# A fused convolution and MLP kernel: the third group's second matmul in seven half products, and the fourth group's second tap made before its first

## The chip, the cores and the metric

The kernel runs on one core of a Trainium2 chip. The metric is the device time in microseconds (us) of one execution. Times of the kernel before are the median of three runs; beside them stands one execution taken by the hardware profiler, and its trace.

A core has engines that run side by side, each with its own instruction queue: TensorE (PE; matmuls into PSUM, eight banks of accumulators), VectorE (DVE), ScalarE (ACT), GpSimd (POOL) and SyncE (SP). SP and POOL also issue DMA transfers here[...]. An engine takes its instructions in order: one that waits holds up all behind it.

## The reference

The input x has 8 sequences of 4224 rows of 192 values. A causal convolution with 7 taps runs along each sequence; the 192 channels form 8 heads of 24, and each head has its own 7 tap weights (a softmax). Then comes a layer normalization over the 192 channels, a matmul to 768 channels, a ReLU, a matmul back to 192, and a residual sum:

```python
w = softmax(weight)                                   # 8 heads x 7 taps
y = einsum('hk,bskhg->bshg', w, windows(x))           # causal, 7 taps
mu, var = mean(y), mean((y - mu) ** 2)                # over the 192 channels
xn = (y - mu) / sqrt(var + 1e-6) * g_ln
out = y + maximum(xn @ w_ch1, 0.0) @ w_ch2            # 192 -> 768 -> 192
```

All is float32.

## The kernel before

**Groups.** The 33792 rows are taken in 18 groups (`groups`, L70). A group is `n` rows on each of 128 partitions: group 0 has 6, group 1 has 8, group 2 has 10, groups 3 to 17 have 16. In the text "the third group" is group 2 and "the fourth" group 3. The buffers are reused: two for loaded rows (`xg`), two for convolved rows (`y`), one each for the transposed rows (`yt`), the hidden layer (`room`), and the results of the second matmul (`cs`).

**What happens to a group.** `load_x` brings its rows in. `first_tap` makes y = tap 0 times x on ScalarE, one instruction for each head (L378). The other taps are one VectorE instruction for each tap and head (`conv`, L403), adding into y. For groups from 4 on, `second_tap` makes tap 1's product on ScalarE into a buffer `tb` (L389), and two accumulating DMAs from POOL add it to y (L392), so that `conv` starts with tap 2. VectorE transposes y in 32x32 blocks (`transpose`, L414) and takes its moments (`moments`, L434); POOL computes the reciprocal root (`root`). `store_y` writes y to the output, and the result of the second matmul is added to the output in memory by an accumulating DMA (`add_to_out`, L891), after ScalarE has scaled it row by row (`scale`, L884).

**Two forms of the matmuls.** In the plain form the first matmul is `up` (six hidden blocks; each is evicted from PSUM by a ScalarE instruction with the ReLU, L509) and the second is `down` (L753), whose results `park` copies to SBUF (L870). In the other form, a matrix product of 2x2 blocks is made of seven half-size products in place of eight, with sums of blocks before and after. `up_mixed` does so for the first matmul from group 3 on: it needs sums of quarters of w1 (`w1sums`, and w12 replaced by w12 - w11) and of the transposed rows (`sums_of_y`; its last two on POOL), and it closes some blocks by copying a partial product to SBUF and adding it there with an accumulating DMA from POOL (`close`, L585). `down_fast` does so for the second matmul: it needs sums of quarters of w2 (`w2sums`), sums of quarters of the hidden layer made by VectorE while the products run (`lower_sum`, `half_sum`, L773), and it copies blocks out on ScalarE (L812). Between the copies ScalarE does other work for later groups, so many pieces behind each copy (`behind`).

**Order.** It is written out by hand; each engine runs its instructions in the order in which the loop from L973 makes them. For groups 0 to 2 that order was: issue the load of group g + 2, `up(g)`, then convolution, transpose, moments and first taps of the groups ahead, then `down(g)`. The sums of w2's quarters stood on VectorE behind group 1's second matmul (L1006), and those of w1's behind group 2's (L1012). Group 2 used `down`; group 3 is the first in the other form for both matmuls. `fast` (L76) says how many rows of a group the second matmul takes in the seven-product form.

**The steps on which the order rests.** An eviction must end before TensorE refills its banks. In `up_mixed` a partial product lies in a part of `room` that a later copy overwrites, so that copy waits for the DMA that adds it. In `down_fast` the second half of the products reads the half sums.

## Time and profile before

| | |
|---|---|
| median of three runs | 962.16 us (959.97 to 962.44) |
| the profiled execution | 960.25 us |
| its span, first to last instruction | 958.5 us |
| granted TensorE clock in it | 0.999 |
| third group's first matmul (L519, 288 instructions of 320 columns) | 80.5 to 100.1 us |
| third group's second matmul (L753, 288 of 320) | 100.1 to 119.6 us |
| fourth group's first matmul (L519, 504 of 256) | 119.6 to 147.4 us |
| fourth group's second matmul (L806, 504 of 256) | 147.4 to 174.9 us |
| DMA: POOL's queue | 100.94 MB, 55.0% of 16 engines' span |
| DMA: SP's queue | 63.31 MB, 17.9% |

How to read it: a row of a timeline gives the start, the length, the engine, the line of the kernel, the operation, output and inputs with their shapes, how many instructions are merged, and in brackets how long the engine had idled and what ended that. Lengths of neighbours overlap a little; the time from one start to the next is what an instruction takes of its engine. A matmul here shows as two instructions. L numbers are lines of the kernel before.

### The profile page before, as it was taken

To read this page: it belongs to the slowest core of one execution; us is meant where nothing else is said; L and a number is where in the kernel's file an instruction comes from. 1 tells how busy PE (TensorE), PEld (TensorE's weight loads), DVE (VectorE), ACT (ScalarE), POOL (GpSimd) and SP (SyncE) were. 2 spreads that over 40 slices of the span, in tenths; PEclk is the share of its full clock that TensorE was granted. 3 is DMA by queue.
4 is the path that set the end of the run, shared out by engine and by line. 5 is a ranking of instruction groups with operands and counts; after the bars stand their busy time and mean duration, and the time that the engine had idled before them with its cause. 6 is when DMAs were issued, how large, how long until landed. Compare 5 with 4: busy or idle time off the path is not lost.

```text
span 958.5 us, 38499 instructions
## 1 busy us (share of the span) xinstructions
PE 948.6 (99%) x17274; PEld 719.5 (75%) x17274; DVE 895.8 (93%) x1510; ACT 686.6 (72%) x1139; POOL 260.9 (27%) x399
## 2 busy tenths in 40 slices
PE   8999999999999999999999999999999999999997
PEld 7886596776869687786958678686867768586787
DVE  8999998999999999999999999999989999999667
ACT  6625578596877959687796958778695877866461
POOL 1005311612135131422216131341315221161400
PEclk9999999999999999999999999999999999999999
DMA  8243887679697887969788796978879697767241
GB/s 221 79 155 112 180 207 216 146 151 265 134 260 142 235 173 158 249 123 276 136 240 163 178 234 118 281 136 243 158 186 216 120 280 141 179 132 129 53 83 68
DMA packets 28394, 166.69 MB, mean 174 GB/s; under 512 B 3397, under 2 KB 4294, under 8 KB 22215
## 3 DMA queue, kind: packets, MB, share of 16 engines
q0 software_dynamic: 21568, 100.94, 55.0%
q1 hardware_dynamic: 6656, 63.31, 17.9%
q8 instruction: 135, 2.21, 0.9%
q14 instruction: 29, 0.24, 0.1%
q10 hardware_dynamic: 6, 0.00, 0.0%
HBM read 38.93 MB, written 50.33 MB: 93 GB/s over the span
## 4 chain that ended last, share of the span: by engine, by line
PE 97%; ACT 1%; DMA 1%; DVE 0%; SPq 0%; issue 0%; ACTq 0%
PE ps L519 48%; PE ps L806 42%; PE ps L753 6%; DMA xg<-in_x_dram 1%; PE ps L322 1%; ACT w L360 0%; ACT room L618 0%; DVE y L898 0%; ACT spare L241 0%; ACT y L378 0%; PE ps L335 0%; SPq L215 0%; ACT room L509 0%; PE ps L350 0%; SPq L210 0%
## 5 line engine op out<-in xcount | busy, mean ns | idle before, releaser
L403 DVE SCALAR_TENSOR_TENSOR y<-xg,taps,y 128x384 f32<-128x384 f32 (+3 forms) x734 | 367.9, 577 | 1.8 <-issue 1.6
L519 PE MATMUL ps<-yt,w 32*128 32x256 f32 (+2 forms) x4104 | 235.7, 379 | 0.4 <-ACT room L509 0.4
L806 PE MATMUL ps<-room,w2sums 128*32 128x256 f32 (+1 forms) x4320 | 235.9, 375 | 0.0
L618 ACT COPY room<-ps 128x1024 f32<-128x1024 f32 (+1 forms) x135 | 175.0, 1296 | 77.2 <-PE ps L519 76.0
L519 PEld LDWEIGHTS ps<-yt,w 32*128 32x128 f32 x4104 | 204.2, 185 | 26.5 <-issue 9.0
L806 PEld LDWEIGHTS ps<-room,w2sums 128*32 128x32 f32 x4320 | 140.5, 110 | 89.7 <-ACT room L631 4.9
L806 PE MATMUL ps<-room,w 128*32 128x256 f32 (+1 forms) x3240 | 181.0, 375 | 0.4 <-issue 0.4
L773 DVE TENSOR_TENSOR room<-room 128x1024 f32<-128x1024 f32 (+1 forms) x135 | 151.6, 1196 | 21.2 <-PE ps L806 20.0
L806 PEld LDWEIGHTS ps<-room,w 128*32 128x32 f32 x3240 | 104.8, 110 | 68.7 <-DVE room L624 5.0
L519 PE MATMUL ps<-ysums,w1sums 32*128 32x256 f32 x2160 | 124.9, 379 | 0.0
L519 PEld LDWEIGHTS ps<-ysums,w1sums 32*128 32x128 f32 x2160 | 108.7, 185 | 11.2 <-ACT room L618 3.6
L812 ACT COPY cs<-ps 128x256 f32<-128x256 f32 (+1 forms) x180 | 66.0, 369 | 42.6 <-PE ps L806 42.6
L884 ACT ACTIVATE ot<-ot,r 128x192 f32<-128x192 f32 x232 | 93.8, 462 | 0.0
L631 ACT ACTIVATE room<-room 128x1024 f32<-128x1024 f32 (+1 forms) x89 | 92.1, 1071 | 0.0
L891 POOL DMA_DIRECT2D out_dram<-ot x40 | 34.2, 1086 | 194.6 <-ACT ot L884 115.7
L378 ACT ACTIVATE y<-xg,taps 128x384 f32<-128x384 f32 (+3 forms) x141 | 72.8, 611 | 9.0 <-DVE st L434 7.6
L434 DVE BATCH_NORM_STATS2 st<-y 128x6 f32<-128x192 f32 x264 | 70.2, 344 | 0.0
L519 PE MATMUL ps<-yt,w1sums 32*128 32x256 f32 x1080 | 65.1, 379 | 0.0
L812 ACT COPY room<-ps 128x256 f32<-128x256 f32 (+1 forms) x90 | 33.6, 373 | 43.9 <-PE ps L806 42.4
L519 PE MATMUL ps<-ysums,w 32*128 32x256 f32 x1080 | 64.5, 376 | 0.0
L618 ACT ACTIVATE room<-ps 128x1024 f32<-128x1024 f32 (+1 forms) x30 | 43.6, 1454 | 27.6 <-PE ps L519 27.6
L389 ACT ACTIVATE tb<-xg,taps 128x384 f32<-128x384 f32 x112 | 61.9, 635 | 0.0
(109 smaller groups left out, 895.3 us busy)
## 6 DMA issues: line engine op xcount, KB each, us to landing
xg<-in_x_dram SPq DMA_DIRECT2D x15, 2112.0 KB, 19.2
room<-room POOLq DMA_DIRECT2D x45, 512.0 KB, 5.3
out_dram<-ot POOLq DMA_DIRECT2D x29, 768.0 KB, 9.5
y<-tb POOLq DMA_DIRECT2D x28, 768.0 KB, 11.4
out_dram<-y SPq DMA_DIRECT2D x13, 1536.0 KB, 10.8
room<-parts_cs POOLq DMA_DIRECT2D x28, 512.0 KB, 6.6
room<-parts_tb POOLq DMA_DIRECT2D x14, 1024.0 KB, 7.6
xg<-in_x_dram SPq DMA_DIRECT2D x1, 1536.0 KB, 8.0
```

Source lines behind the costliest of these rows:

```text
L378: nc.scalar.mul(y[g][:, 0:n, cs], xg[g][:, 0:n, cs], taps[:, h, 0:1])
L389: nc.scalar.mul(tb[g][:, 0:n, cs], xg[g][:, 1 : 1 + n, cs], taps[:, h, 1:2])
L403: nc.vector.scalar_tensor_tensor(out=y[g][:, 0:n, cs], in0=t[:, k : k + n, cs], scalar=taps[:, h, k : k + 1], in1=y[g][:, 0:n, cs], op0=AL ...
L434: nc.vector.bn_stats(out=sums[g][:, j, :], in_=y[g][:, j, :])
L519: nc.tensor.matmul(banks[:, q, i * w : i * w + w], right[rows, c, P * i : P * i + P], left[rows, :, c, :], start=(first and c == 0 and i = ...
L618: nc.scalar.activation(dst, src, AF.Relu) if relu else nc.scalar.copy(dst, src)
L631: nc.scalar.activation(c, c, AF.Relu)
L753: nc.tensor.matmul(bank[C * q : C * q + C, 0:w], w2[:, f, C * c : C * c + C], left, start=(f == 0), stop=(f == NF - 1),)
L773: nc.vector.tensor_tensor(a[:, *dst, f], a[:, *left, f], a[:, *right, f], op=op)
L806: nc.tensor.matmul(dst[C * q : C * q + C, 0:w], right[:, f, C * c : C * c + C], left[:, f, q], start=(first and f == PAIR), stop=(f == PAI ...
L812: nc.scalar.copy(to[:, c], dst[:, 0:w].rearrange("p (j t) -> p j t", t=t))
L884: nc.scalar.mul(ots[g][:, j, :], ots[g][:, j, :], rstd[g][:, j : j + 1])
```

## The change

The third group's second matmul goes over to the seven-product form (`fast[2]`), with one ScalarE piece behind each copy of its first four products. Its first matmul keeps the plain form; only the layout in which its result is written differs.

- The sums of w2's quarters and most of w1's leave VectorE: ScalarE writes a negated quarter and accumulating DMAs from POOL add the others (`between`, between the hidden blocks of groups 1 and 2). Only w12 - w11 stays on VectorE.
- The second tap of group 2 and that of heads 0 to 5 of group 3 are made on ScalarE and added by DMA (`add_second_tap`). For group 3 it is made before the first tap, into a free end of `room`, while group 1's hidden blocks are evicted; the DMA moves 144 of each row's 192 channels.
- The loads of groups 3, 4 and 5 move: group 3's ahead of the stores of group 1 on SP, group 4's and 5's to POOL's queue. The load of group 5 and the store of group 3's y come behind the third group's second matmul.
- First taps of group 4 are made between hidden blocks of group 2; its second tap is made during the second matmul of group 2.
- The scaling of groups 0 and 1 and their additions to the output are regrouped. Group 2's result is finished as the later groups' are, inside the next group's first matmul.

```diff
@@ -75,6 +75,7 @@
 
     fast = {g: groups[g][2] if g >= 3 else 0 for g in range(NG)}
     fast[NG - 1] = J - 5
+    fast[2] = groups[2][2]
     NFAST = max(fast.values())
     T = C // 2
 
@@ -129,7 +130,7 @@
 
     xg = {}
 
-    def load_x(g, queue=nc.sync):
+    def load_x(g, queue=nc.sync, pad=True):
         b, j0, n = groups[g]
         t = xpool.tile([P, J + PAD, D], F32, tag="xg", name=f"xg{g}")
         xg[g] = t
@@ -157,7 +158,8 @@
                     tensor=x.tensor, offset=(b * S - PAD) * D, ap=[[R * D, P], [1, (PAD + n) * D]]
                 ),
             )
-            nc.gpsimd.memset(t[0:1, 0:PAD, :], 0.0)
+            if pad:
+                nc.gpsimd.memset(t[0:1, 0:PAD, :], 0.0)
             return
         nc.gpsimd.memset(t[0:1, 0:PAD, :], 0.0)
         for p0, p1 in ((16, P), (1, 16)):
@@ -382,17 +384,28 @@
     def second_tap(g, heads=(0, H)):
 
         n = groups[g][2]
-        if heads[0] == 0:
+        if heads[0]:
+            pass
+        elif g == 2:
+            part = upool.tile([P, 3 * HJ * CH * C], F32, tag="ys", name="tb2")
+            tb[g] = part[:, 0 : n * D].rearrange("p (j d) -> p j d", d=D)
+        elif g == 3:
+            tb[g] = room[:, (NF * NQ * C - D) * J :].rearrange("p (j d) -> p j d", d=D)
+        else:
             tb[g] = bpool.tile([P, J, D], F32, tag="tb", name=f"tb{g}")
         for h in range(*heads):
             cs = slice(h * GRP, h * GRP + GRP)
             nc.scalar.mul(tb[g][:, 0:n, cs], xg[g][:, 1 : 1 + n, cs], taps[:, h, 1:2])
         if heads[1] == H:
-            for j1, j2 in ((0, n // 2), (n // 2, n)):
-                nc.gpsimd.dma_start(
-                    out=y[g][:, j1:j2].rearrange("p j d -> p (j d)"),
-                    in_=tb[g][:, j1:j2].rearrange("p j d -> p (j d)"), accum_op=ALU.add,
-                )
+            add_second_tap(g)
+
+    def add_second_tap(g, upto=H):
+        n = groups[g][2]
+        for js in (slice(0, n // 2), slice(n // 2, n)):
+            ends = [v[:, js, 0 : upto * GRP] for v in (y[g], tb[g])]
+            if upto == H:
+                ends = [v.rearrange("p j d -> p (j d)") for v in ends]
+            nc.gpsimd.dma_start(out=ends[0], in_=ends[1], accum_op=ALU.add)
 
     def conv(g, k0=1, k1=K, heads=(0, H)):
         n = groups[g][2]
@@ -498,7 +511,7 @@
             dst = ht[g][:, f]
             src = src.rearrange("p q (j t) -> p q j t", t=C)
         elif width(g) == C:
-            dst = ht[g][:, :, f // FC, f % FC].rearrange("p h q j t -> p q h (j t)")
+            dst = of_products(g)[:, :, f // FC, f % FC].rearrange("p h q j t -> p q h (j t)")
             src = src.rearrange("p q (h w) -> p q h w", h=2)
         else:
             dst = ht[g][:, :, f // FC, f % FC].rearrange("p h q j t -> p q j h t")
@@ -522,11 +535,47 @@
                         stop=(last and c == left.shape[2] - 1), skip_group_check=split,
                     )
 
+    def between(g, f):
+
+        b11, b12, b21, b22 = quarters_of_w2()
+        d0, d1, d2, d3 = [w2sums[:, v] for v in range(4)]
+        w11, w12, w21, w22 = quarters_of_w1()
+        e1, e2, e3 = [w1sums[:, v] for v in range(3)]
+        if g == 1:
+            negative, added = {
+                0: ([(d2, b22), (d0, b11)], [(d2, b12), (d0, b12)]),
+                1: ([(d1, b12), (d3, b11)], [(d1, b22), (d3, b21)]),
+                2: ([(e1, w12)], []),
+                5: ([], [(d1, b11), (d3, d2)]),
+            }.get(f, ([], []))
+            for to, of in negative:
+                nc.scalar.mul(to, of, -1.0)
+            for to, of in added:
+                add_by_dma(to, of)
+            if f in (3, 4, 5):
+                second_tap(3, heads=[(0, 2), (2, 5), (5, 6)][f - 3])
+        elif g == 2:
+            if f == 0:
+                add_by_dma(e2, w12)
+                add_by_dma(e1, w11)
+                add_by_dma(e3, w21)
+                scale(0, 0, groups[0][2])
+                add_to_out(0, 0, groups[0][2])
+                nc.gpsimd.memset(xg[4][0:1, 0:PAD, :], 0.0)
+            elif f < 3:
+                m = groups[1][2]
+                scale(1, m * (f - 1) // 2, m * f // 2)
+                if f == 2:
+                    add_by_dma(e1, w22)
+                    add_by_dma(e3, e2)
+                    add_to_out(1, 0, m)
+            else:
+                first_tap(4, heads=[(0, 2), (2, 4), (4, 7)][f - 3])
+
     def up(g):
 
 
         n = groups[g][2]
-        scaled = (0, 1) if g == 2 else ()
         hidden_tile(g)
         for f in range(NF):
             banks = take_set()
@@ -537,14 +586,7 @@
                 join_words(w2flat, *words_2)
             if g == 0 and f < 2:
                 first_tap(1, heads=(H // 2 * f, H // 2 * (f + 1)))
-            if 1 <= f <= 4:
-                for s in scaled:
-                    m = groups[s][2]
-                    scale(s, m * (f - 1) // 4, m * f // 4)
-                    if f % 2 == 0:
-                        add_to_out(s, m * (f - 2) // 4, m * f // 4)
-
-
+            between(g, f)
 
     def quarters_of_w1(f0=0, f1=FC):
         return [
@@ -819,17 +861,24 @@
         b = quarters_of_w2()
         c11, c21 = cs[:, 0:CH, 0], cs[:, 0:CH, 1]
         c12, c22 = cs[:, CH:NC, 0], cs[:, CH:NC, 1]
-        if g + 2 < NG:
+        if g == 2:
+            work += [lambda h=h: first_tap(4, heads=(h, h + 1)) for h in range(7, H)]
+            work += [lambda h=h: second_tap(4, heads=(h, h + 1)) for h in range(H)]
+        elif g + 2 < NG:
             work += [
                 lambda tap=tap, h=h: tap(g + 2, heads=(h, h + 1))
                 for tap in (first_tap, second_tap) for h in range(H)
             ]
-        product(0, a[:, 0, 0], b[0], c11, True, 3)
-        product(1, a[:, 1, 0], w2sums[:, 2], c22, True, 2)
-        product(1, a[:, 1, 1], w2sums[:, 3], c21, False, 2)
-        product(1, a[:, 0, 1], b[2], None, True, 3)
+        behind = (1, 1, 1, 1) if g == 2 else (3, 2, 2, 3)
+        product(0, a[:, 0, 0], b[0], c11, True, behind[0])
+        product(1, a[:, 1, 0], w2sums[:, 2], c22, True, behind[1])
+        product(1, a[:, 1, 1], w2sums[:, 3], c21, False, behind[2])
+        product(1, a[:, 0, 1], b[2], None, True, behind[3])
         if g + 1 < NG:
             transpose(g + 1)
+            if g == 2:
+                b11, b12 = quarters_of_w1()[0:2]
+                nc.vector.tensor_tensor(b12, b12, b11, op=ALU.subtract)
         half_sum(g, (1, 1), (1, 1), (1, 0), ALU.add)
         half_sum(g, (0, 0), (1, 1), (0, 0), ALU.add)
         half_sum(g, (0, 1), (0, 1), (1, 1), ALU.subtract)
@@ -845,6 +894,8 @@
         product(0, a[:, 0, 1], b[3], c12, False)
         if g + 1 < NG:
             sums_of_y(g + 1, nc.gpsimd)
+            if g == 2:
+                store_y(g + 1, nc.gpsimd)
             moments(g + 1)
         else:
             finish_fast(g, 0, flat, cs, parts)
@@ -972,49 +1023,52 @@
 
     for g in range(NG):
         mixed, last = g in MIXED, g + 1 == NG
-        if g + 2 < NG:
-            load_x(g + 2)
+        if g + 2 < NG and g not in (1, 2):
+            load_x(g + 2, nc.gpsimd if g == 3 else nc.sync)
         if mixed:
             work = up_mixed(g, ahead(g), pending)
             pending = iter(())
         else:
             up(g)
-        if not fast[g]:
-
-            if g:
-                conv(g + 1)
-                transpose(g + 1)
-            else:
-                early = CH * C // GRP
-                conv(1, heads=(0, early))
-                transpose(1, 0, CH)
-                conv(1, heads=(early, H))
-                transpose(1, CH, NC)
-            if g < 2:
-                store_y(g + 1)
-                moments(g)
-            first_tap(g + 2)
-            if g == 2:
-
-                second_tap(g + 2)
-                store_y(g + 1, nc.gpsimd)
+            work = []
+        if g == 0:
+            early = CH * C // GRP
+            conv(1, heads=(0, early))
+            transpose(1, 0, CH)
+            conv(1, heads=(early, H))
+            transpose(1, CH, NC)
+            load_x(3)
+            store_y(1)
+            moments(0)
+            moments(1)
+            first_tap(2)
+            second_tap(2)
+            next(root(0, True))
+            w11, w12, w21, w22 = quarters_of_w1()
+            nc.scalar.mul(w1sums[:, 1], w22, -1.0)
+        elif g == 1:
+            conv(2, 2)
+            transpose(2)
+            store_y(2)
+            first_tap(3)
+            add_second_tap(3, 6)
+            load_x(4, nc.gpsimd, pad=False)
+            nc.scalar.mul(w1sums[:, 2], w11, -1.0)
+        elif g == 2:
+            conv(3, 2, 5, heads=(0, 6))
+            lower_sum(2)
+            conv(3, 5, K, heads=(0, 6))
+        if g < 2:
             down(g)
             park(g)
             if g == 1:
+                moments(2)
                 finish(0)
-                next(root(0, True))
-                sums_of_quarters([w2sums[:, v] for v in range(4)], *quarters_of_w2())
-                moments(2)
                 next(root(2, True))
+                conv(3, heads=(6, H))
                 finish(1)
-            elif g == 2:
-                b11, b12, b21, b22 = quarters_of_w1()
-                sums_of_quarters([b12] + [w1sums[:, v] for v in range(3)], b11, b12, b21, b22)
-                sums_of_y(3, nc.vector)
-                finish(2)
-                moments(3)
             continue
-        if g + 2 < NG:
+        if g > 2 and g + 2 < NG:
             store_y(g + 1)
         results = down_fast(g, work)
         if last:
```

## The prediction

> **What bounds the kernel now.** I read the page's busy shares and chain first, then the chain in order of time, then each engine's timeline from 20 to 182 us, then the DMA issues.
>
> ```profile
> PE 948.6 (99%) x17274; PEld 719.5 (75%) x17274; DVE 895.8 (93%) x1510; ACT 686.6 (72%) x1139; POOL 260.9 (27%) x399
> ...
> PE 97%; ACT 1%; DMA 1%; DVE 0%; SPq 0%; issue 0%; ACTq 0%
> ```
>
> The chain that ends last is TensorE for 97% of the span. In order of time (start, length):
>
> ```profile
> 64.84 15.68 PE ps L753 x288
> 80.52 19.59 PE ps L519 x288
> 100.11 19.52 PE ps L753 x288
> 119.63 27.82 PE ps L519 x504
> 147.45 27.44 PE ps L806 x504
> ```
>
> From 31.0 us on it never stops, so a TensorE microsecond removed is a microsecond won, if nobody comes late. 100.11 to 119.63 is the third group's second matmul: 288 instructions of 320 columns. The fourth group already has the cheap form (L806, 504 instructions). VectorE is almost as full:
>
> ```profile
> 50.92 18.28 DVE L403 SCALAR_TENSOR_TENSOR y<-xg,taps,y 128x240 f32<-128x240 f32 x48
> 69.31 2.18 DVE L414 STREAM_TRANSPOSE yt<-y 128x1920 f32<-128x1920 f32 x1
> ...
> 81.36 25.49 DVE L403 SCALAR_TENSOR_TENSOR y<-xg,taps,y 128x384 f32<-128x384 f32 x48
> 106.96 3.38 DVE L414 STREAM_TRANSPOSE yt<-y 128x3072 f32<-128x3072 f32 x1
> ...
> 159.04 10.31 DVE L773 TENSOR_TENSOR room<-room 128x1024 f32<-128x1024 f32 x9 [1.05 <-PE ps L806]
> ```
>
> Each transpose precedes its matmul (80.52, 119.63) by 9 us; that room is what the change spends. The last row is work of the seven-product form: nine half sums, begun when TensorE has finished the third product. ScalarE's closest place is in the fourth group's first matmul:
>
> ```profile
> 139.88 1.86 ACT L618 COPY room<-ps 128x2048 f32<-128x2048 f32 x1
> ...
> 142.34 1.87 ACT L618 COPY parts_tb<-ps 128x2048 f32<-128x2048 f32 x1 [0.25 <-PE ps L519]
> ```
>
> The first copy ends at 141.74; TensorE refills those banks at 142.09. Room: 0.35 us. POOL's transfers there (columns: count, KB, us from issue to landing):
>
> ```profile
> out_dram<-y POOLq DMA_DIRECT2D x1, 1536.0 KB, 18.2
> y<-tb POOLq DMA_DIRECT2D x1, 768.0 KB, 15.0
> ...
> room<-room POOLq DMA_DIRECT2D x1, 512.0 KB, 7.2
> ```
>
> [...] the three 512 KB additions issued at 123.9, 128.0 and 129.3 land at 131.6, 134.1 and 136.6, one every 2.4 us. [...] no run here shows a 576-byte run. [...] The trace agrees on GpSimd's side: its small root operations take 0.21 us until 81.3 and 0.45 us beside the taps after it; the taps stay at 0.53 us, so I charge VectorE nothing.
>
> **The product itself.** Seven products of 72 instructions, 160 columns wide, replace 288 of 320. Pitches of L753: 19.52/288 = 67.8 ns (320 columns), 54.4 (256), 41.1 (192): 1.1 ns plus 0.2086 per column, so 34.4 at 160. 504 x 34.4 = 17.35 us. Gain **2.17 us**, the only TensorE time removed.
>
> **VectorE until the half sums.** Unchanged until 49.39. Then, from the timeline's rows: 14 moments 3.58; taps 2 to 6 of the third group 40 x 0.383 = 15.33 (8 go to ScalarE); transpose 2.10; moments 2.61; six transposes 1.59; taps of heads 6 and 7 of the fourth group 12 x 0.533 = 6.40; six transposes 2.02: at 83.0. Heads 0 to 5: 18 x 0.533 = 9.60; three lower sums of 640 elements 3 x 0.74 = 2.21 (between 1.14 at 1024 and 0.80 at 704); 12 taps 6.40; transpose 3.30; b12 less b11 1.35: **105.9**. The first half sum may start when the third product is out, 100.11 + 3 x 2.48 = 107.5, and three of them (2.2) must end before the fourth is (110.0). VectorE has 1.6 + 0.26 us to spare. The weight sums (7.1 us on VectorE at 75.0 and 110.3) are gone to ScalarE and DMA; this pays for the twelve sums. I cost it at nothing; without cover, one for one.
>
> **Two additions by DMA feed that row.** Third group: ScalarE's eight products end at 44.2, two 480 KB additions issue by 46.1; 512 KB takes 4.5 to 5.7, so about 52, wanted at 53.0. Fourth group: ScalarE ends its first-tap products at 70.6 (evict at 64.91, nine products of 0.515), and 2 x 590 KB are wanted at 83.0, harmful from 84.9. Contiguous, at 221 GB/s (1.57 MB in 7.1 us), it is 5.3 us plus about 3: 79. But these are 576-byte runs, 128 for each of 16 engines. Lower end 79; [...] upper end, a run as dear as the trace's 4 KB one (305 ns), 39 us: 113. I take 82: nothing.
>
> **ScalarE.** Third load: wanted at 60.8 between two evictions; moved ahead of eight stores on SP, issued at 48.5, it needs about 8.7 as now: 57.2, free. Fifth load, on POOL behind the 576-byte additions: data until about 89, the memset behind it until 91, wanted at 95.0; TensorE would feel it from about 98. The root and three weight additions stand in POOL's queue between (some 10 + 3 us from 75), free. In the second matmul itself: the sixth eviction ends at 101.31, three products 1.54, so the first copy starts at 102.86; each slot is a copy (0.18) and one product (0.515). The fourth copy ends at 105.26; TensorE wants its bank at 104.99. **0.3 us** lost; bounds 0 and 0.6.
>
> **The transfers kept out.** The store of y3 (1.5 MB) and the load for the sixth group (2.1 MB, issued on SP at 106.93 now) follow POOL's two sums. VectorE: half sums 107.8 + 6.6, additions 0.75, sums 1.9 = 117.1; POOL's two sums 2 x 1.92; store issued at 121, load at 122. They stand in the same queue ahead of the three closing additions of the next matmul. The y4 additions issue at 109.5 and are through by 121 (11.3 as at 165.8). The 3.74 MB: at 380 to 420 GB/s (cf. 417 and 422 in 74 to 78 us) 8.9 to 9.8, so until 131.1 to 132.0; three additions, 7.1, and about 0.5 to complete: third lands at 138.7 to 139.6. TensorE starts the stage at 119.63 - 2.17 + 0.3 = 117.8, so the copy at 139.88 now, whose room the third addition still reads, comes at 138.0 and may wait until 138.3 or 138.4. I take **0.9 us** lost; lower end 0, upper 5.9 if 254 GB/s holds (3.73 MB between 107 and 129.5 beside 1.57 MB of additions). Behind that copy wait ScalarE's own relus and evictions, and TensorE for them.
>
> Next late if this stall goes: the relus waiting for additions 4 and 5 (144 against 144.1), then VectorE, whose 0.87 to 1.46 us of idling before L624 stay. After this group the order is as before.
>
> **Sum.** -2.17 + 0.3 + 0.9 = about **-1.0 us**. Profiled execution before: 958.5 span, 960.25 time (1.75 around it). After: 957.5 and 959.3. The median shown, 962.16, is 1.9 above the profiled time; on it 961.2. A measurement of this kernel tells 0.3%, 2.9 us, from no change.
>
> **The cases.**
> 1. Forecast, small stalls, net -0.2 to -1.8: 961.2, own range 960.2 to 962.2. 45%.
> 2. No stall: POOL's transfers at the upper rate, ScalarE's copy in time. For it: 0.3 and 0.9 are the ends of long sums. Against: both margins come out negative. -2.2: 960.0. 15%.
> 3. Slower, the 576-byte additions: VectorE's taps stand at 83.0 until they land, the half sums come late, and TensorE stops before the fifth product. It decides from 84.9, one for one; with 140 ns a run 18 + 3 us, landing at 91.6, 6.7 us lost: -2.2 + 0.3 + 6.7 = +4.8, and the stage behind it moves along, so the closing additions cost nothing more: 967.0. For: no row shows such runs[...]. 17%.
> 4. Slower, the closing additions: at 254 GB/s 5.9 us lost, +4.0: 966.2. For: that is the mixed rate now; against: then other additions ran among them. 15%.
> 5. ScalarE stands before an eviction for the third or fifth load: 2 to 8 us late, about 965. Against: 3 and 4 us of room. 8%.
>
> Faster by over 0.3% needs more than TensorE loses; only scatter (runs before: 959.97 to 962.44) gives it: 0.10. Within: 0.57, cases 1 and 2 and the mild ends of 3 to 5. Slower: 0.33. The range 959.2 to 967.0 leaves out the scatter below and the worse half of 3 and 4.
>
> **What would show it.** Right: 504 instructions of 160 columns in 17.3 us; VectorE waiting for TensorE, not the reverse, before its first 640-element sum near 107.5; a TensorE gap of 0.3 us after the second product; the sixth group's load landing near 132 and a gap under 1.5 us near 138. Wrong: VectorE idle at 83 for a DMA (case 3), a gap over 4 us near 138 (case 4), ScalarE idle near 60 or 95 (case 5), or any longer TensorE gap before 175.

## The result and the profile after

| | before | after |
|---|---|---|
| median | 961.20 us (22 runs, 959.97 to 963.49) | 963.83 us (22 runs, 961.08 to 967.32) |
| the profiled execution | 960.25 us | 966.46 us |
| third group's second matmul | 19.5 us | 24.3 us |
| fourth group's first matmul | 27.8 us | 29.3 us |

The ratio is 1.0029, with an interval of 1.0019 to 1.0039: the change costs 2.6 us where I had forecast a gain of 1.0. The profiled execution is on the slow side of its own scatter; the sums below are made against its own time.

The page's busy shares are nearly those of before (TensorE 98% in place of 99%). Its chain:

```profile
PE 97%; ACT 1%; issue 1%; DMA 1%; DVE 0%
```

One share has grown: "issue", from 0% to 1% of the chain. It is time in which an engine waited for nothing that the profile shows. TensorE's timeline gives its place (start, length):

```profile
99.30 2.65 PE L848 MATMUL ps<-room,w 128*32 128x160 f32 x72
...
109.42 0.74 PE L848 MATMUL ps<-room,w2sums 128*32 128x160 f32 x14
113.44 6.23 PE L848 MATMUL ps<-room,w2sums 128*32 128x160 f32 x128 [3.27 <-issue]
120.76 0.32 PE L848 MATMUL ps<-room,w2sums 128*32 128x160 f32 x1 [1.10 <-issue]
...
123.60 2.87 PE L532 MATMUL ps<-yt,w 32*128 32x256 f32 x48
...
127.81 2.85 PE L532 MATMUL ps<-ysums,w1sums 32*128 32x256 f32 x43 [0.80 <-issue]
```

Until 109.4 the new stage goes at the pace that was forecast: a product starts 2.47 us after the one before it (99.30, 101.77), the third alone 0.26 us later than that. Then TensorE stops three times, for 3.27, 1.10 and 0.80 us, and no engine or transfer is named. In four-microsecond windows (busy time of PE, PEld, DVE, ACT and POOL, then granted clock, share of the DMA engines, GB/s):

```profile
108.00:112.00 4.00, 2.17 (x63) 1.78 (x55) 4.00 (x6) 0.46 (x1) 1.25 (x3) 1.00 0.94 150
112.00:116.00 4.00, 2.56 (x48) 2.55 (x51) 3.97 (x8) 0.41 (x2) 1.45 (x2) 0.74 0.96 184
```

and in the kernel before:

```profile
108.00:112.00 4.00, 4.00 (x68) 1.91 (x61) 3.97 (x3) 2.44 (x6) 2.21 (x3) 1.00 0.99 300
112.00:116.00 4.00, 4.00 (x68) 1.91 (x64) 3.93 (x4) 0.42 (x1) 0.14 (x1) 1.00 0.89 257
```

Two things stand there. The clock that TensorE was granted falls after the long stop (0.74): its next 128 matmuls take 6.23 us instead of 4.4. And the DMA engines are full; but in these two windows they were as full before, beside wide matmuls and without a stop. Over the whole stretch they have become much fuller. The same columns for three longer windows, before:

```profile
70.00:96.00 26.00, 26.00 (x428) 17.98 (x424) 25.93 (x63) 14.20 (x28) 13.16 (x40) 1.00 0.40 132
96.00:121.00 25.00, 25.00 (x380) 13.40 (x376) 24.72 (x34) 14.20 (x29) 9.53 (x12) 1.00 0.83 181
121.00:147.00 26.00, 26.00 (x480) 23.73 (x476) 24.54 (x52) 19.95 (x18) 5.14 (x6) 1.00 0.81 191
```

and after:

```profile
70.00:96.00 26.00, 26.00 (x428) 18.05 (x423) 24.20 (x56) 13.50 (x27) 15.45 (x27) 1.00 1.13 206
96.00:121.00 25.00, 20.53 (x487) 18.08 (x483) 24.75 (x46) 12.72 (x30) 14.69 (x16) 0.93 1.06 189
121.00:147.00 26.00, 25.20 (x474) 23.22 (x473) 19.59 (x38) 16.74 (x18) 4.56 (x6) 1.00 0.89 241
```

Share times length, added over the three rows, is the time for which all 16 DMA engines would be busy: 52 us before and 79 us after, in a stretch of 77 us. (A share over 1, such as the 1.13, means that the records of packets overlap.)

VectorE's rows and the closing additions, to be held against those of before:

```profile
84.06 9.62 DVE L416 SCALAR_TENSOR_TENSOR y<-xg,taps,y 128x384 f32<-128x384 f32 x18 [1.80 <-DMA y<-room]
...
107.07 6.71 DVE L815 TENSOR_TENSOR room<-room 128x640 f32<-128x640 f32 x9
```

```profile
room<-room POOLq DMA_DIRECT2D x3, 512.0 KB, 7.2
```

VectorE did idle at 82.3 us, 1.8 us long, for the 576-byte additions. But it is free for the half sums at 106.96, and the third product, which they wait for, is out only then (the fourth starts at 106.98): VectorE was just not late. The closing additions take 7.2 us to land, as before, and cost nothing, since TensorE came to them late.

**Where TensorE stops.** The page lists a kind of packet that I had passed over:

```profile
q8 instruction: 137, 2.24, 0.9%
```

2.24 MB in 137 packets is 16 KB each. TensorE has 35151 instructions in this trace (loads of weights, matmuls and the few others), and 35151 / 137 is about 257. So a packet looks like one block of 256 TensorE instructions. Counting TensorE's instructions up to each stop over 0.6 us between 95 and 135 us, worked out from the trace's records:

```
before instruction   stops at us   for us   packet of q8 runs     TensorE resumes after its end
3777 = 14*256+193    109.87        3.57     111.02 to 111.98      1.46 us
4033 = 15*256+193    119.37        1.40     118.55 to 119.50      1.26 us
4289 = 16*256+193    126.64        1.17     125.55 to 126.47      1.34 us
```

Each stop lies exactly 256 instructions behind the one before it, whatever product is running, and each ends 1.3 to 1.5 us after a packet. A fourth, of 0.86 us, comes at 506 us, again before a multiple of 256 plus 193 (70 of them). (These times run from one instruction's start to the next, so they hold the idle of the timeline and about 0.3 us more.)

### The profile page after: what moved, and what is told of

It is laid out like the page before. It is cut to its first block, busy times and chain, and to the rows that moved or that the text cites. A ratio compares the mean times of both kernels' runs of the same rounds, so it can differ in the third digit from the quotient of the medians.

```text
span 964.5 us, 38995 instructions
## 1 busy us (share of the span) xinstructions
PE 949.7 (98%) x17490; PEld 728.5 (76%) x17490; DVE 893.2 (93%) x1505; ACT 699.4 (73%) x1172; POOL 286.5 (30%) x417
## 3 DMA queue, kind: packets, MB, share of 16 engines
q8 instruction: 137, 2.24, 0.9%
## 4 chain that ended last, share of the span: by engine, by line
PE 97%; ACT 1%; issue 1%; DMA 1%; DVE 0%
PE ps L532 48%; PE ps L848 43%; PE ps L795 4%; PE ps L367 1%; PE ps L324 1%; DMA out_dram<-y 0%; ACT y L380 0%; ACT room L660 0%; ACT w L362 0%; ACT room L522 0%; DVE y L949 0%; PE ps L333 0%; PE ps L337 0%; ACT spare L243 0%; DMA room<-in_weight_dram 0%
## 5 line engine op out<-in xcount | busy, mean ns | idle before, releaser
L416 DVE SCALAR_TENSOR_TENSOR y<-xg,taps,y 128x384 f32<-128x384 f32 (+3 forms) x720 | 361.9, 579 | 3.7 <-DMA y<-room 1.8
L848 PE MATMUL ps<-room,w2sums 128*32 128x256 f32 (+2 forms) x4608 | 248.8, 372 | 5.0 <-issue 4.8
L848 PEld LDWEIGHTS ps<-room,w2sums 128*32 128x32 f32 x4608 | 150.6, 111 | 97.2 <-issue 6.0
L848 PE MATMUL ps<-room,w 128*32 128x256 f32 (+2 forms) x3456 | 188.6, 370 | 0.1
L815 DVE TENSOR_TENSOR room<-room 128x1024 f32<-128x1024 f32 (+2 forms) x147 | 160.6, 1167 | 20.4 <-PE ps L848 20.3
L848 PEld LDWEIGHTS ps<-room,w 128*32 128x32 f32 x3456 | 111.7, 110 | 68.8 <-DVE room L666 5.0
L854 ACT COPY cs<-ps 128x256 f32<-128x256 f32 (+2 forms) x192 | 69.7, 366 | 44.2 <-PE ps L848 44.2
L854 ACT COPY room<-ps 128x256 f32<-128x256 f32 (+2 forms) x96 | 35.4, 368 | 55.5 <-PE ps L848 48.2
L408 POOL DMA_DIRECT2D y<-tb x30 | 26.6, 1032 | 148.7 <-ACT room L854 110.1
L398 ACT ACTIVATE tb<-xg,taps 128x384 f32<-128x384 f32 (+1 forms) x120 | 66.1, 629 | 0.0
```

The source lines that it names most:

```text
L398: nc.scalar.mul(tb[g][:, 0:n, cs], xg[g][:, 1 : 1 + n, cs], taps[:, h, 1:2])
L416: nc.vector.scalar_tensor_tensor(out=y[g][:, 0:n, cs], in0=t[:, k : k + n, cs], scalar=taps[:, h, k : k + 1], in1=y[g][:, 0:n, cs], op0=AL ...
L815: nc.vector.tensor_tensor(a[:, *dst, f], a[:, *left, f], a[:, *right, f], op=op)
L848: nc.tensor.matmul(dst[C * q : C * q + C, 0:w], right[:, f, C * c : C * c + C], left[:, f, q], start=(first and f == PAIR), stop=(f == PAI ...
L854: nc.scalar.copy(to[:, c], dst[:, 0:w].rearrange("p (j t) -> p j t", t=t))
```

## The experiments

**The theories.** A: TensorE starves for its own instructions. Its blocks come over the same 16 DMA engines as the data (0.9% of their span in q8's row); a block lasts 128 matmuls, by the measured starts 4.4 us at 160 columns (34.3 ns each, 2.47 us / 72) against 7.0 at 256 (54.4) and 8.7 at 320 (67.8), and beside full engines the next block comes too late. B: TensorE waits for data, for a reason that the trace can't name. Later came C: the transfers that the change adds and moves cost by themselves, where they stand ahead of the closing additions.

Each profiled run is summed up here by the two stages concerned, from TensorE's timeline (start of a stage to start of the next), with the start of the second part of the first matmul (of group 0), after which TensorE is busy in the kernel before but for one stop of 0.7 us. What is lost in other stages is not in the last column:

```
                   that start   third's 2nd   fourth's 1st   both
before                31.00        19.52         27.82       47.34
after                 30.26        24.30         29.31       53.61
again                 31.07        23.35         27.86       51.21
early_w1              30.27        22.58         28.78       51.36
no_out                30.54        17.67         31.91       49.58
no_w1                 30.40        17.57         32.22       49.79
plain_down            32.83        19.52         28.81       48.33
plain_down_b          33.16        19.52         29.56       49.08
pool_sums             32.67        24.74         28.72       53.46
pool_sums_sp          30.75        24.86         29.07       53.93
no_w1_sp5             30.61        22.50         27.90       50.40
after_sp5             31.02        22.58         29.32       51.90
no_out_load_late      30.42        20.02         27.86       47.88
load_late             32.71        23.80         27.86       51.66
```

**The change once more.** No edit.

> The changed kernel once more, unaltered. Theory A (TensorE runs out of instructions: its instruction blocks are fetched by the same DMA engines that the accumulating transfers keep full): every TensorE idle time over 0.6 us between 95 and 135 us begins after the same number of TensorE instructions modulo 256 as in the first trace (193), whatever its length. Theory B (TensorE waits for data: the half sums, or a sum of w2's quarters that a DMA makes): idle times begin at the first matmul of a product.

963.87 us. Stops before instructions 3777 and 4033 again, 2.93 and 1.11 us; the third one fell under the 0.6 us counted. The places are fixed by the count of instructions and the lengths vary, which goes with A. This run also closes the sum: the two stages are 3.87 us longer than before (51.21 against 47.34), and 963.87 is 3.6 above the 960.25 of before.

**Transfers without any change to the computation.** The kernel before, with six additions of 0.75 MB between buffers that nothing reads any more, under the last narrow matmul (176 columns) at the end of the kernel. A one-element copy on POOL, not shown here, makes them start with that matmul:

```diff
+        if last:
+            old, new = [xg[k].rearrange('p j d -> p (j d)') for k in (g - 1, g)]
...
+            for k in (0, 1, 0, 1, 0, 1):
+                part = slice(2112 * k, 2112 * k + 1536)
+                nc.gpsimd.dma_start(out=old[:, part], in_=new[:, part], accum_op=ALU.add)
```

> The kernel before, with six additions by DMA between two buffers that nobody needs any more (0.75 MB each), started when the last group's seven-product matmul (176 columns, 38 ns a matmul, DMA nearly idle) begins; they touch nothing that it reads. Theory A: one or more TensorE idle times of 1 to 4 us appear between 925 and 945 us, 256 instructions apart, and the time is 963 to 969 us. Theory B: no idle time, 961 us.

963.80 us, ratio 1.0033 (1.0019 to 1.0046). In TensorE's timeline of this kernel:

```profile
935.83 0.77 PE L806 MATMUL ps<-room,w2sums 128*32 128x176 f32 x14
937.70 5.25 PE L806 MATMUL ps<-room,w2sums 128*32 128x176 f32 x129 [1.10 <-issue]
```

The stop is before instruction 33729 = 131 x 256 + 193. The packet that ends it starts 4.38 us late, counted as under "How late a block may come"; the same packet in the kernel before starts 0.56 us late. From 932 to 940 us the DMA engines' share is 1.00, where it was 0.00 and 0.01 before. TensorE's data are those of before and nothing that it reads waits for the added transfers: full DMA engines alone stop it. For the stops with no releaser, A is shown and B falls. (This execution took 962.42 us; the stage with the stop is 1.5 us longer than before. The median lost more, and its other executions left no trace.)

**Less to transfer beside the narrow matmul.** Two runs, each leaving a part out: `no_out` the first two groups' additions to the output, `no_w1` the five additions that make w1's sums.

```diff
-                add_to_out(0, 0, groups[0][2])
...
-                    add_to_out(1, 0, m)
```

> The changed kernel without the additions of the first two groups' results to the output in memory (1.3 MB; this part of the output is left out). Theory A: 108 us of DMA engine time, 6.8 us of all 16, leave the backlog before 111 us; the gap shrinks or goes, 960 to 962 us. Theory B: 963 to 964 us, gap unchanged.

```diff
-                add_by_dma(e2, w12)
-                add_by_dma(e1, w11)
-                add_by_dma(e3, w21)
...
-                    add_by_dma(e1, w22)
-                    add_by_dma(e3, e2)
```

> The changed kernel without the five additions by DMA that make w1's sums (3 MB; those sums are left unfinished). Theory A: 267 us of DMA engine time, 16.7 us of all 16, leave the backlog, the idle times at instruction blocks between 99 and 118 us go, and what stays is the closing additions' wait of 1 to 1.6 us near 138 us: 960 to 961 us. Theory B: 963 to 964 us.

962.35 us (ratio 1.0012, 1.0002 to 1.0021) and 963.27 us (1.0024, 1.0014 to 1.0035). The narrow stage is now what the product promised, 17.7 and 17.6 us without a stop. TensorE in `no_w1`, its transfers, and ScalarE:

```profile
99.45 2.65 PE L843 MATMUL ps<-room,w 128*32 128x160 f32 x72
...
117.02 2.87 PE L532 MATMUL ps<-yt,w 32*128 32x256 f32 x48
...
120.88 2.85 PE L532 MATMUL ps<-ysums,w1sums 32*128 32x256 f32 x43 [0.46 <-issue]
...
143.85 2.87 PE L532 MATMUL ps<-yt,w1sums 32*128 32x256 f32 x48 [2.39 <-ACT room L655]
```

```profile
room<-room POOLq DMA_DIRECT2D x3, 512.0 KB, 14.0
```

```profile
141.93 1.87 ACT L655 COPY room<-ps 128x2048 f32<-128x2048 f32 x1 [2.78 <-DMA room<-room]
```

But the time isn't won. The next matmul is 4.1 and 4.4 us longer: the closing additions take 14.0 us to land where they took 7.2, ScalarE's copy waits 2.78 us for them, TensorE 2.39 us for the copy, and 0.8 us goes in a stop for a block before instruction 4289 (0.6 to 0.7 each in three of them in `no_out`). That is the wait for which the prediction had charged 0.9 us, shown once TensorE comes on time. Both medians lie above what A had forecast.

**The additions earlier.** The five additions of w1's quarters made between 34 and 50 us instead, with the negations they need:

```diff
+        if g == 0 and f > 2:
+            to, of, more = [(e2, w22, w12), (e1, w12, w11), (e3, w11, w21)][f - 3]
+            nc.scalar.mul(to, of, -1.0)
+            add_by_dma(to, more)
```

> The changed kernel with the five additions by DMA that make w1's sums (0.6 MB each) moved from 81-110 us to about 34-50 us, where the DMA engines stand idle. Theory A: the DMA engines' backlog behind the third group's second matmul goes, no TensorE idle time over 0.6 us is left in 99-118 us, and the time falls to 959 to 961 us. Theory B: the half sums and w2's sums are where they were, so the 3.3 us gap stays and the time is 963 to 964 us. A third outcome: the gap goes, and the closing additions of the fourth group, now early enough to be late, cost 1 us or more near 138 us.

965.45 us, ratio 1.0043 (1.0030 to 1.0055): worse than the change, where I had expected it to be better. TensorE stops in the second group's first matmul, at 49.1 us before instruction 1473 = 5 x 256 + 193 and at 56.6 us 256 instructions later; these are matmuls of 256 columns. VectorE waits for the third group's tap additions, and from then on it is late:

```profile
49.80 7.19 PE L532 MATMUL ps<-yt,w 32*128 32x256 f32 x128 [0.36 <-issue]
```

```profile
55.52 15.26 DVE L416 SCALAR_TENSOR_TENSOR y<-xg,taps,y 128x240 f32<-128x240 f32 x40 [3.16 <-DMA y<-tb]
```

```profile
113.41 5.09 PE L846 MATMUL ps<-room,w2sums 128*32 128x160 f32 x142 [2.21 <-DVE room L813]
120.64 0.32 PE L846 MATMUL ps<-room,w2sums 128*32 128x160 f32 x1 [2.14 <-issue]
```

The change spends nearly all of VectorE's room on its twelve sums, so a transfer that is 3 us late there reaches TensorE, which waits 2.21 us for the half sums.

**The moves without the product.** The third group's second matmul is plain again and everything else stays, in two runs:

```diff
-    fast[2] = groups[2][2]
...
+        if g == 2:
...
+            down(2)
+            park(2)
+            sums_of_y(3, nc.gpsimd)
+            store_y(3, nc.gpsimd)
```

> The changed kernel with its third group's second matmul put back to the plain form (288 matmuls of 320 columns), all moved transfers kept. Theory A (instruction blocks fetched late): a block of 256 TensorE instructions lasts 8.7 us there in place of 4.4, so the same transfers leave no idle time over 0.6 us between 99 and 119 us, and the time is 961 to 962.5 us: the 2.2 us are not won, and nothing much is lost. Theory B (the moved sums and taps come late): idle times stay, 965 us or more.

> A second look at the kernel that keeps every move of the change and has the third group's second matmul in its plain form. If its loss against the kernel before lies in the fourth group's first matmul (28.8 us against 27.8 in the first look), that is there again, 0.7 to 1.5 us over, whatever the start of the run; if it lay in a late start (TensorE 1.8 us later at 33 us in the first look), this run, started at the usual 30.3 to 31.5, comes to within 1 us of the kernel before, 961 to 962.5.

963.93 us (ratio 1.0037, 1.0022 to 1.0053) and, in one further execution, 964.70; the first had been expected at 961 to 962.5. No stop from 99 to 121 us, as A says for 320 columns beside the same transfers. Yet by the medians the moves alone lose as much as the whole change. Both of the places asked about show a loss. The fourth group's first matmul takes 1.0 and 1.7 us more than before (in the first trace 0.5 us of it is a stop for a block before instruction 4289; in the second TensorE idles 1.4 us behind the closing copy). And TensorE's start is 1.8 and 2.2 us late. The late start lies at 10 to 18 us. There TensorE waits longer for VectorE and its first products then run slowly; in the first of the two:

```profile
10.54 0.88 PE L332 MATMUL ps<-room 128*128 128x384 f32 x2 [1.65 <-DVE raw L998]
12.62 3.45 PE L323 MATMUL ps<-xg,room 128*128 128x144 f32 x14 [1.19 <-DMA xg<-in_x_dram]
```

In the kernel before the same two rows show a wait of 0.99 and a length of 1.95 us. `pool_sums` and `load_late` start late too, though none of these edits touches that part. The traces' clock records tell what the four have in common: in each the granted clock is at half for 3.41 us, from a moment between 12.0 and 13.5 us, and in none of the other eleven traces does it fall there. Half of 3.41 is 1.7 us, which is the late start of these four (1.7 to 2.2 us) but for 0.5 us at most. The wait for VectorE just before is 1.5 to 1.8 us in the four and 1.0 to 1.3 in the others. Why VectorE comes later is open, and so is how often a kernel's other executions start like this: so the medians do not tell the moves' own cost from it.

**The sums by GpSimd instead of DMA.** w1's and w2's sums as subtractions on POOL, and in the second run the store of y3 also put on SP:

```diff
+                for to, p, m in ((e1, w12, w11), (e1, w22, e1), (e3, w21, e1)):
+                    nc.gpsimd.tensor_tensor(to, p, m, op=ALU.subtract)
```

> The sums of w1's and w2's quarters made by GpSimd (eight subtractions of about 2.7 and 0.8 us) in place of ScalarE's negations and eleven additions by DMA; everything else as in the changed kernel. Theory A: as without w1's additions, 960 to 961 us, with w2's 143 us of DMA engine time gone too. A rival for this kernel: [...] VectorE comes up to 8 us late to the half sums, and the time is over 964 us.

> The same, and the fourth group's rows stored by SP as soon as they are convolved (near 102 us), so that they don't stand ahead of the closing additions. If those additions' wait near 138 us comes from the store and the load in their queue: the wait goes, 0.5 to 1.5 us faster than with the store behind POOL's sums, less what the store's 4 us of full DMA engines cost in instruction fetches during the narrow matmul.

967.24 us (1.0064, 1.0051 to 1.0078) and 968.87 us (1.0082, 1.0064 to 1.0101). With fewer transfers the first has no stop for a block, but:

```profile
85.61 15.20 DVE L416 SCALAR_TENSOR_TENSOR y<-xg,taps,y 128x384 f32<-128x384 f32 x18
```

```profile
116.36 7.72 PE L835 MATMUL ps<-room,w2sums 128*32 128x160 f32 x144 [4.25 <-DVE room L802]
```

The 18 taps take 15.20 us beside three GpSimd subtractions instead of 9.62, the half sums come late, and TensorE waits 4.25 us. That is 0.84 us a tap, where the 12 taps before them take 6.40 us and the 12 behind 6.43, 0.53 us each: VectorE loses 5.6 us. In the kernel before, beside GpSimd's small root operations, the taps had stayed at 0.53 us. By what the subtractions slow the taps is not shown. The second run was to be 0.5 to 1.5 us faster than the first and is 1.6 slower: TensorE waits 4.26 us for the half sums there too, and stops twice for a block, 0.9 us from start to start.

**The sixth group's load in another place.** It stands on POOL's queue ahead of the closing additions in the change. Put on SP, where it was before, without (`no_w1_sp5`, which leaves out what `no_w1` does) and with w1's additions:

```diff
-            load_x(g + 2, nc.gpsimd if g == 3 else nc.sync)
+            load_x(g + 2)
```

> The five additions of W1's quarters are left out (the fourth group's first matmul computes with unfinished sums), and the load for the sixth group goes to SP's queue, as in the kernel before, instead of POOL's queue behind the store of y3. Against the same kernel with that load on POOL (963.3 us, TensorE idle 2.4 us behind the eviction at 144 us). Theory that the closing additions are late because they stand behind 3.7 MB in their own queue: only 1.5 MB are ahead of them now, they land at most 9 us after their issue (14.0 for the first before), the idle is under 0.5 us and the time 960.5 to 961.5. Rival, that the DMA engines are simply full then, whatever the queue: the load, issued on SP near 107 us, takes its share all the same, the additions take over 11 us, the idle stays over 1.5 us and the time at 963. Instruction blocks: the load now runs beside the second half of the second matmul with the y4 additions, and one gap of 0.5 to 1.5 us may come near 118 to 121.

> The changed kernel with nothing left out, the load for the sixth group on SP's queue instead of POOL's. Theory of instruction blocks: the narrow matmul has still more transfers beside it, so TensorE's gaps at instructions 3777, 4033 and 4289 stay or grow, 4 to 8 us in all, and the time is 964 to 967. Theory that the queue behind the store is what costs: the time falls to 961 to 962 although the gaps are there.

964.57 us (1.0028, 1.0019 to 1.0036) and 965.41 us (1.0041, 1.0030 to 1.0052). In `no_w1_sp5` the closing additions are quick again, and TensorE doesn't wait behind them:

```profile
room<-room POOLq DMA_DIRECT2D x3, 512.0 KB, 5.1
```

Landing and wait are as the theory of the queue said; its time, 960.5 to 961.5, is missed by 3 us. (TensorE comes to the copy 5 us later than in `no_w1`, so the landing tells more than the missing wait.) The load now runs beside the narrow matmul, and TensorE stops there:

```profile
110.97 4.55 PE L843 MATMUL ps<-room,w2sums 128*32 128x160 f32 x128 [0.47 <-issue]
117.74 0.48 PE L843 MATMUL ps<-room,w2sums 128*32 128x160 f32 x1 [2.22 <-issue]
```

I had expected one stop of 0.5 to 1.5 us and got two, 0.8 and 2.5. Then the load behind the closing additions, with and without the first groups' additions to the output:

```diff
+            if g == 3:
+                load_x(5, nc.gpsimd)
```

> Leaves out the first two groups' additions to the output, as an earlier run did (that one: 962.35 us, no gap in the narrow matmul, three gaps of 0.6 to 0.7 us at 120 to 136 us, TensorE idle 1.6 us behind the eviction at 142 us), and issues the sixth group's load behind the closing additions, instead of ahead of them. If instruction blocks and closing additions are the whole of the loss, the idle behind the eviction goes to under 0.4 us, the gaps at 120 to 136 shrink since the load no longer runs there, and the time is 959.5 to 961, below the kernel before (961.5) by what the product saves less the 0.4. Rival, a third cost that no gap shows: the idle goes and the time stays above 961.5. Risk: ScalarE needs the load for the fifth group's products from about 150 us; issued near 141 us and 10 us long it is just in time, later costs TensorE up to 1 us.

> The changed kernel complete, with the sixth group's load issued behind the closing additions of the fourth group's first matmul. Theory of instruction blocks: the gaps in the narrow matmul stay (2.5 to 5 us with the slow clock behind them), since the additions by DMA and the output additions there are untouched; TensorE is then late, the closing additions cost nothing, and the gap near 127 us shrinks with the load gone from there: 962 to 963.5, about 1 us better than the change, no better than the kernel before. Rival, that the load's place is the main cost: 960 to 961.5.

962.26 us (1.0009, 0.9994 to 1.0024) and 966.04 us (1.0058, 1.0032 to 1.0085). The fourth group's first matmul takes 27.86 us in both, 0.04 over that of before. In `load_late` that proves little, since `again`, where TensorE is late as well, has it too. In `no_out_load_late` the last closing addition lands at 136.45 us, where it landed at 141.75 in `no_out`, and the copy at 139.84 doesn't wait for it. But the risk named came, larger than named. ScalarE gets its rows too late (2.7 us) and TensorE waits for it at 158 us, and a block is late once more at 114.6; in `no_out_load_late`:

```profile
116.65 0.32 PE L846 MATMUL ps<-room,w2sums 128*32 128x160 f32 x1 [1.77 <-issue]
...
160.45 2.79 PE L846 MATMUL ps<-room,w2sums 128*32 128x256 f32 x24 [2.44 <-ACT cs L852]
```

With this wait the fourth group's second matmul takes 31.56 and 29.62 us instead of 27.44, outside the table's sum. `load_late` missed both of its forecasts, 962 to 963.5 and 960 to 961.5.

So no run shows the product's 2.17 us as a gain. What the table shows is an exchange: where the narrow stage runs at 17.6 us, the next one takes 32; where the next takes 27.9, the narrow one takes 20 to 24. No kernel has the two under the 47.34 us of before. No version here beats the kernel before.

**How late a block may come.** Worked out from the records: in all fifteen traces no packet of q8 starts earlier than 284 instructions before the place where TensorE would stop for it. At 17.2 ns an instruction (160 columns) 284 of them last 4.9 us. Of that the packet takes 0.95 us and the way from its end to the first instruction 1.35, so it may start 2.6 us late; at 256 columns (27.2 ns) it is 5.4, at 320 columns 7.3. These are estimates from the traces' numbers. Beside the stops in narrow stages:

```
                    before instr.   packet late by   less 2.6   stop, us
after                   3777            6.07           3.5        3.57
again                   3777            5.62           3.0        2.93
after_sp5               3777            5.60           3.0        2.99
load_late               3777            5.93           3.3        2.99
no_out_load_late        4033            4.57           2.0        2.07
no_w1_sp5               3777            3.25           0.7        0.77
no_w1_sp5               4033            5.76           3.2        2.52
early_w1                4033            4.79           2.2        2.44
```

"Late by" counts from the moment at which TensorE passed the 284th instruction before the stop. That this is the moment of the request is assumed from the smallest lead seen. Left out are later stops before 4033 (in `after`, `again`, `load_late` and `pool_sums_sp`), where an earlier stop or a slow clock lies within the count and makes it larger.

The lag itself was there before: in the trace of before its median is 2.6 us, and at 114.7 us, for the block of instruction 3777, it is 4.1, hidden by matmuls of 320 columns. By this estimate a narrow stage would have stopped for 1.5 us there beside the old transfers; the added ones lengthen the lag to 5.6 to 6.1. One stop of this kind, 0.73 us before instruction 23489 = 91 x 256 + 193, at 659 us, stood in the kernel before too, where the prediction has TensorE never stop from 31.0 us on.

## Why the prediction was wrong, point by point

- **The product, 2.17 us: right.** It does what was worked out: 17.57 us without a stop (`no_w1`) against 19.52, with 0.27 us of it lost behind the second product, and the 2.47 us between products are the 2.48 used.
- **"A TensorE microsecond removed is a microsecond won, if nobody comes late": this step failed.** Somebody came late who is in no row of waits: TensorE's own instructions. The sum has no term for it, so it put the cost at nothing. Against the 17.57 us it is 5.8 us in `again` and 6.7 in the profiled run, of which 4.0 and 5.0 are stops and the rest the lower clock; the profiled run has 1.2 us more of it in the stage behind.
- **Costing the added transfers by the engine that waits for them: failed with it.** I asked of each addition when it lands and who wants it, and charged nothing for those in time. All were in time, or harmless: the 576-byte ones (a median of 89 ns a run in this trace; the 82 us taken for their landing was an estimate of mine that no run had shown) landed at 83.97 us, let VectorE idle 1.8 us and left it just in time for the half sums. What they took was the DMA engines' time, which rose from 52 to 79 us in a stretch of 77, and that has another user: the 137 packets of q8, 16 KB for every 257 or so of TensorE's instructions. In the kernel before they cost TensorE one stop, of 0.73 us; beside narrow matmuls and full DMA engines the change has stops of 3.57 and 1.40 us. The prediction has no term for these packets.
- **VectorE in time: right, with luck.** The room of 1.6 us was used up: VectorE is free at 106.96 in place of 105.9, and TensorE, 0.8 us earlier than reckoned, has the third product out at 107.0. In `again` it waits 0.44 us for TensorE.
- **ScalarE's copies, the third and fifth loads: right.** The third product starts 0.26 us late behind the fourth copy, where 0.3 was charged, and ScalarE waits for neither load.
- **The closing additions: mechanism right, size wrong.** 0.9 us with bounds of 0 and 5.9; measured 2.4 where TensorE is on time (`no_w1`), 1.2 in `no_out`, 0 to 1.4 in the plain form. The mis-sized term is the store and the load ahead of them: in `no_w1` the load landed at 134.4 us, not at 131.1 to 132.0, and the last addition at 141.8, not at 138.7 to 139.6. (Two readings were off by little: the additions land 2.5 us apart, not 2.4, and the window named for 254 GB/s, 107 to 129.5, shows 268.) In the change itself nothing of this shows, because the starvation had already made TensorE late: two losses that don't add.
- **The cases.** None of those that end slower is the one that came. The last sign named, any longer TensorE gap before 175 us, is what was seen. That the time lies inside the range is luck: other mishaps had widened it.

## What to carry to other kernels

A narrower or shorter instruction uses up the instruction stream faster: before making matmuls shorter, work out how long 256 instructions last (here 8.7 us at 320 columns, 4.4 at 160), and read the DMA share in that very window (here about 1): a lag of 4.1 us that the matmuls of 320 columns hid would by the estimate above have stopped those of 160 for 1.5. Work moved from a busy engine to DMA is not free because its landing is on time; add up the DMA engines' time over the stretch, and treat a sum near the stretch's length (here 79 us in 77) as a second bound. A stop with no releaser ("issue"), at a fixed count of instructions (here 256), is the sign of it.

## What the runs showed of the hardware

- TensorE's instruction blocks, as `after` shows them: 137 packets of 16 KB for 35151 instructions, 0.9 to 1.0 us a packet at the stops, TensorE going on 1.3 to 1.5 us after the packet's end, with an allowance of about 2.6 us at 160 columns (estimate above).
- A stop can cost more than its length. After 3.27 us of idling the granted clock is at half for 3.41 us by the trace's clock records, and 128 matmuls took 6.23 us instead of 4.4; after 2.22 us in `no_w1_sp5` the last product took 4.3 instead of 2.5. The length of the idling alone doesn't decide it: after 2.69 us in `load_late` and 1.77 us in `no_out_load_late` the matmuls kept their pace. What else decides it is not shown.
- The same half clock, once for 3.41 us near 12 us, makes an execution start about 1.7 us later (`plain_down`, `plain_down_b`, `pool_sums`, `load_late`).
